# Second half of the tokens, and the state model's input, transposed straight from DRAM, under a rewritten order of work

## The chip, the cores and the metric

The kernel runs on one core of one Trainium2 chip. A core has engines with instruction queues of their own: TensorE (PE; its weight loads are listed as PEld), VectorE (DVE), ScalarE (ACT), GpSimd (POOL) and SyncE (SP), which here issues nearly all DMAs. Each queue is worked off in order, and the engines meet through semaphores. The time is the device time of one execution in microseconds; a profiled execution gives a span from the first to the last instruction and a time of its own.

## The reference

Two independent models, whose outputs are laid side by side (2048 tokens, 448 columns each). The first is local attention: 16 heads of 28 columns, each token looking at 8 tokens at distances 0, 2, ... 14.

```python
qkv = (x @ wqkv).reshape(B, S, 3, H, Dh)            # S = 2048, H = 16, Dh = 28
idx = pos[:, None] - 2 * arange(8)[None, :]
logits = einsum("bhsd,bhswd->bhsw", q, k[idx]) * Dh ** -0.5   # masked where idx < 0
a = einsum("bhsw,bhswd->bhsd", softmax(logits), v[idx]).reshape(B, S, D) @ wo
```

The second is a state model with 448 complex states, a diagonal recurrence over the tokens:

```python
h = Lam_bar * h + x[t] @ B_bar.T
y = 2 * real(h @ Cmat.T) + x * Dskip
```

## The kernel before

The kernel is one stream of some 560 named steps, written out by hand in the string `ORDER` (L32 to L61). Each step calls a function of the same name; the loop at L885 emits them in that order, so the order of the string is the order of every engine's queue. `@` gives the PSUM banks of a step; a trailing `.` has an eviction done by ACT, a trailing `=` by DVE. Large letters are mostly work for PE, small letters for the others.

Attention. Tokens are in two units `u` of 1024, each of two halves `s` of 512. PE wants x with columns on the partitions, as `xT`: 448 columns are three tiles of 128 and a tail of 64. For unit 0, x is loaded by rows into `xbuf` (as `xnA`) and PE transposes it: XI (first 512 tokens), XA and XH (second 512 tokens; XH is the tail), evicted by xi, xa and xh. For unit 1, x is loaded by rows too (L155 to L157), and four DMA transposes (L171 to L173) go from there into `xT`. The two halves' tails share one tile: half 0 on partitions 0 to 63, half 1 on 64 to 127.

QK(u, m, k) multiplies `xT` with a feature group `m` of `wq`: even m is query, odd m is key, m = 6 what is left of both (collected in `wq6` by POOL). k = 0 is the three full tiles of both halves, six matmuls; k = 1 the pair of tails; whichever comes first begins the bank. QS does a group for one half alone, as the first matmuls of the kernel. qk and qh evict. V_ and v do the values. P (L379, DVE) multiplies queries with shifted keys, E_ (PE) sums the products per head; lt, TD (a DMA transpose), sma, smb, smc are the softmax. AL, al, ad, sp bring the weights into banded form by way of a scratch in DRAM, into `PT`; AV, av, W_, w, ow make and store the attention output.

State model. Tokens are in chunks of 4. `Bn` (rows of B) is transposed by one DMA into `BT` (step BD). `xTB` is x with columns on the partitions, for two pairs of positions in a chunk (`a`) and 512 chunks. Before, x is loaded by rows into `xnB`, packed so that a pair of tokens is seven tiles of 128 (`x_load`, L164 to L169 and L179), and step xt (L694) transposes 128 chunks at a time into `xTB`, which lies in `xbuf`, over the rows of A. BU(g, jp, k) multiplies `BT` with the pair jp of `xTB`. BR, z, UP and y carry the state inside a chunk, sa, sb and sd scan over the chunks (DVE), DN, dn, H_ and h bring the states back, C and c make the output and oc stores it, from `xnA`, again over `xbuf`. XR reloads x by rows into `xnB` for the Dskip term (xd). ty, tf and ts make the tables of sines, the steps pa to pg the constants, rb the rotations, ca and cs scale C.

SP's queue is: first loads of x and `wq` (L141 to L153), unit 1's rows, the first x_load, unit 1's four transposes, Bn, the second x_load; then from `ORDER` BD, the four xt, TD0, LC, XR, CD, TD1 and what follows. ACT issues three small loads and one piece of the weights' tail (`w_half` with `eng=ACT`).

Of the kernel before, what the change touches and what calls it, by code (L numbers as in the profile page):

```python
# [16 lines left out]
NT = 16  # L17
# [21 lines left out]
P051 v411. ts06 v410. P060 QK110@46 ts16 BD v110. ts26 P061 QK101 ty3 QK151@72 QK111 qk100. E_05 rb0 qk101. E_06  # L39
qk110. QK150 tf4 lt00 P100 V_401@31 qk151. V_501@45 V_500 rb3 qk150. xt1 ts04 P101 lt01 QK120@27 ts14 qk111. tf3  # L40
v501. QK140@06 xt0 v500. P110 ts03 QK121 P111 QK141 qk120. QK161@54 V_400 qk140. xt3 P120 ts13 qk121. QK160 v400.
P121 qk141. v401. E_10@20 xt2 ts23 P130 E_11 ts24 V_510@73 qh101. P131 qh110. qh111. E_12 TD0 qh100. P140 E_13 hc1
V_511 P141 v511. v510. LC BU301@61 BU201@45 P150 BU300 sma0 BU200 OZ z30. XR BU400@37 z20. P151 smb0 BU000@64 P160
BR31 P161 BU001 ci1. BU401 E_14 z00. E_15 ci2= CD1 z40. E_16 rb1 z31. BR21 BR01 lt11 BU500@63 ci0= CD2 z21. smc0
z01. BU211@10 ci3. CD0 BU311@54 BU501 BU310 lt10 z50. CD3 BR32 BR41 BU210 z41. xd3 TD1 z32. BR51 xd2 BR22 AL0@2 z51.
BR33 z22. BU100@67 al0= z33. xd0 ca3 ad0 BU011@53 BU111@12 BU101 sma1 OP pm3 BU010 z10. pm0 wo UP3 AL1@6 cs3 smb1
BR11 xd1 BR02 BU110 z02. smc1 z11. BR03 al1. BR12 BU510@57 z03. ad1 z12. pm1 sp0 ca6 UP0 BR13 BU600@61 z13. y3. y0.
cs6 UP1 BR23 BU601 y1. z23. BU511 sa0 BU411@43 z60. BR52 pm4 ca1 BU410 sp1 sb0 BR61 z52. BR42 BU611@26 ca2 BU610 pm2
sd0 z61. AX@5 z42. BR53 BR62 AL2@1 ax= z53. z62. cs1 DN0@4 UP5 adx UP2 al2. DN1@5 BR43 dn0 BR63 y2. dn1 AL3@2 ad2
z63. sa2 H_10@1 y5. H_20@4 z43. H_11@0 al3. UP6 UP4 H_21@5 y6. H_00@7 ad3 y4. H_01@2 AV011@6 ca4 h21 spx AV010@3 h20  # L50
AV030@5 h01 av011. sp2 AV000@4 av010. cs2 AV020@6 av030. sb2 AV021@2 av000. AV001@3 av020. AV031@5 sd2 av001. W_00@4
sp3 av031. av021. W_20@6 ca5 h11 DN2@3 W_01@5 h00 DN3@2 dn2 w20. W_10@0 dn3 w01. sa4 ow20 W_11@7 ow01 W_21@3 w11.
w10. H_03@6 h10 H_02@2 w00. H_22@5 cs4 W_30@7 w21. ow00 sb4 H_23@0 ow21 H_13@1 w30. W_31@4 ow10 ca0 ow30 h13 AV100@3
ow11 h03 AV110@7 sd4 AV111@1 av110. AV131@6 av111. AV101@7 h02 av131. AV121@1 sa6 av101. AV130@6 av121. AV120@2 cs0
av130. DN5@7 av100. cs5 W_71@1 av120. dn5 W_61@6 w31. sb6 w71. h23 H_05@3 ow31 W_51@2 w61. ow71 ow61 W_41@7 w51= h05
H_15@4 ow51 H_25@1 W_50@0 h15 sd6 DN4@6 W_60@2 w50. w41. W_40@3 ow50 w60= ow41 DN6@4 C32@0 w40. ow60 dn6 dn4 ow40
h25 H_06@7 H_16@2 H_04@3 h06 H_12@4 H_14@6 h04 W_70@1 c32 H_24@7 C31@3 h22 oc32 w70= h12 C33@0 ow70 c31 h14 oc31
H_26@5 C30@1 c33 h26 oc33 h24 C02@4 c30 oc30 C20@3 c02 C00@6 c20 h16 oc20 CH0@0 c00 C01@5 oc00 C11@7 c01 ch0 oc01
C12@1 oh0 oc02 C13@4 C22@3 C03@2 c22 c12 oc22 c13 C21@6 oc12 c11 oc13 oc11 C10@5 c21 c03 oc21 CH1@0 oc03 c10 ch1
# [4 lines left out]
def kernel(  # L64
# [54 lines left out]
    xbuf = keep.tile([128, NT * D], BF16, tag="xbuf")  # L119
    xnA = xbuf.rearrange("p (t d) -> p t d", d=D)  # L120
# [34 lines left out]
    xA1 = xbuf[:, 8 * D:].rearrange("p (t n) -> p t n", n=2 * D)  # L155
    for d0, d1, b, c in ((0, D, 8, 0), (D, 512, 12, 384), (512, 896, 12, 0)):
        SP.dma_start(xA1[:, :, d0:d1], xA_r[:, b:b + 4, c:c + d1 - d0])  # L157


    xnB = keep.tile([128, 4, T, D], BF16, tag="xnB")  # L160
    xP = xnB.rearrange("p c j d -> p c (j d)").rearrange("p c (a n) -> p c a n", a=2)
    xB_r = B_x[0].rearrange("(q p h a b) d -> h p q a b d", q=2, p=128, h=2, a=2)

    def x_load(hh):  # L164
        for d0, d1, b, c in ((0, D, 0, 0), (D, 512, 1, 384), (512, 896, 1, 0)):
            for q in range(2):
                SP.dma_start(xP[:, 2 * hh + q, :, d0:d1], xB_r[hh, :, q, :, b, c:c + d1 - d0])

    x_load(0)  # L169

    xT = s2.tile([128, 2, 7, 512], BF16, tag="xT")  # L171
    for t in range(4):
        SP.dma_start(xT[:, 1, :, 128 * t:128 * t + 128], xA1[:, t], transpose=True)  # L173

    Bn = s2.tile([128, G, 512], BF16, tag="Bn")
# [3 lines left out]
    x_load(1)  # L179
# [154 lines left out]
    @op  # L334
    def QK(u, m, k):
        p = two("qk", u, m)
        part(("qk", u, m), k,
             [[(p[s][:], wqk(m, slice(64 * s, 64 * s + 64), 3), xT[64 * s:64 * s + 64, u, 3]) for s in range(2)]] if k else
             [[(p[s][:], wqk(m, slice(0, 128), kt), xT[:, u, 4 * s + kt]) for s in range(2)]
              for kt in range(3)])  # L340

    @op
    def QS(m, s):

        p = ps()
        pp.setdefault(("qk", 0, m), {})[s] = p
        for kt in range(3):
            PE.matmul(p[:], wqk(m, slice(0, 128), kt), xT[:, 0, 4 * s + kt], start=(kt == 0), stop=False)  # L348
        PE.matmul(p[:], wqk(m, slice(64 * s, 64 * s + 64), 3), xT[64 * s:64 * s + 64, 0, 3], start=False, stop=True)
# [341 lines left out]
    xTB = xbuf.rearrange("p (a b c) -> p a b c", a=2, b=7)  # L691

    @op
    def xt(cb):  # L694

        SP.dma_start(xTB[:, :, :, 128 * cb:128 * cb + 128].rearrange("p a b c -> p (a b) c"),
                     xnB[:, cb].rearrange("p j d -> p (j d)"), transpose=True)
# [222 lines left out]
```

## Time and profile before

| | |
|---|---|
| time, median of 3 runs | 133.71 us (133.06 to 136.21) |
| time of the profiled execution | 132.89 us |
| its span | 130.7 us |
| PE busy | 125.4 us, 1067 matmuls |
| DVE busy | 113.4 us |
| ACT busy | 88.8 us |
| HBM read, written | 11.69 MB, 6.37 MB |
| granted clock | 1.00 |

The profile's page gives busy times over the span and in 40 slices of 3.27 us, each digit the busy share in tenths. The timeline lists instructions in order with start, time taken, engine, line, tile written and read, number of them, and, in square brackets, idle time before them with what ended it. Matmuls overlap, so that one of 0.38 us lets the next start after about 0.21. SPq rows are instructions that issue DMAs; their time is that of the issue, not of the transfer.

### The profile page before, as it was taken

The page shows a single profiled execution, that of the slowest core. Times are in us where ns is not written, and L with a number is a line of the kernel's source. Part 1 is how long each engine was busy: PE and PEld are TensorE (multiplying, and loading weights), DVE is VectorE, ACT ScalarE, POOL GpSimd, SP SyncE. Part 2 cuts the span into 40 slices and gives each one's busy share as a digit, 9 for nine tenths or more (in the row PEclk, how much of TensorE's full clock was granted, in tenths as well). Part 3 has the DMA queues.
Part 4 walks back from the last instruction along what each step waited for, and adds up shares of the span by engine and source line. Part 5 has one row for each costly group of instructions (what it writes and reads, how often), then busy time and mean ns, then how long its engine had stood idle before and what let it go on. Part 6 is the DMA issues. An engine that isn't in the chain of part 4 may idle for free.

```text
span 130.7 us, 2869 instructions
## 1 busy us (share of the span) xinstructions
PE 125.4 (96%) x1067; PEld 62.2 (48%) x1067; DVE 113.4 (87%) x206; ACT 88.8 (68%) x185; POOL 19.8 (15%) x37
## 2 busy tenths in 40 slices
PE   6999999999999999999999999999899999999991
PEld 6543443434233334334454356854575555565550
DVE  5679999999999999999999899999997999752282
ACT  1779999999978996995979999997497300000000
POOL 6802000000000000200799920000000000000000
PEclk9999999999999999999999999999999999999999
DMA  3997989899999998999786999999412332213043
GB/s 116 238 207 174 326 230 167 197 197 258 139 259 210 212 200 187 310 303 209 209 200 222 185 169 293 255 179 185 141 54 70 105 105 94 87 55 103 0 146 118
DMA packets 47780, 23.24 MB, mean 178 GB/s; under 512 B 35639, under 2 KB 46711, under 8 KB 47767
## 3 DMA queue, kind: packets, MB, share of 16 engines
q1 hardware_dynamic: 47560, 23.03, 78.3%
q8 instruction: 8, 0.13, 0.4%
q10 hardware_dynamic: 207, 0.04, 0.2%
q14 instruction: 5, 0.04, 0.1%
HBM read 11.69 MB, written 6.37 MB: 138 GB/s over the span
## 4 chain that ended last, share of the span: by engine, by line
PE 80%; ACT 7%; DMA 6%; SPq 3%; issue 1%; DVE 0%; ACTq 0%
PE ps L244 38%; PE ps L807 15%; PE ps L547 6%; PE ps L534 5%; PE ps L391 5%; ACT ctmp L684 4%; DMA out_dram<-ya 3%; PE ps L722 3%; DMA wq<-in_A_wqkv_dram 3%; PE ps L788 3%; ACT Z L114 2%; SPq L128 2%; PE ps L348 1%; PE ps L827 1%; PE ps L395 1%
## 5 line engine op out<-in xcount | busy, mean ns | idle before, releaser
L379 DVE TENSOR_TENSOR pr<-qf,kf 128x2048 bf16<-128x2048 bf16 x24 | 28.7, 1236 | 0.1
L244 PE MATMUL ps<-xbuf,BT 128*128 128x512 bf16 (+1 forms) x112 | 23.6, 380 | 0.0
L244 PE MATMUL ps<-xT,wq 128*128 128x512 bf16 (+1 forms) x96 | 20.6, 380 | 0.1
L807 PE MATMUL ps<-Cw,Z 128*128 128x448 bf16 x105 | 20.5, 352 | 0.0
L114 ACT CAST Z<-ps 128x512 bf16<-128x512 f32 (+1 forms) x35 | 15.8, 520 | 3.0 <-PE ps L722 1.5
L813 DVE TENSOR_TENSOR xbuf<-ps,xnB 128x448 bf16<-128x448 f32 x15 | 9.0, 620 | 7.6 <-PE ps L807 7.5
L244 PEld LDWEIGHTS <-BT 128*128 128x128 bf16 (+1 forms) x112 | 8.9, 97 | 12.6 <-issue 3.5
L807 PEld LDWEIGHTS <-Z 128*128 128x128 bf16 x105 | 10.3, 98 | 9.4
L793 DVE TENSOR_TENSOR Z<-ps,Z 128x512 bf16<-128x512 f32 x21 | 13.7, 680 | 0.2 <-PE ps L788 0.2
L547 PE MATMUL ps<-wo,oT 128*128 128x448 bf16 x64 | 13.6, 353 | 0.0
L244 PEld LDWEIGHTS <-wq 128*128 128x128 bf16 (+1 forms) x96 | 7.8, 97 | 11.0 <-issue 2.3
L244 PE MATMUL ps<-wq,xT 128*128 128x448 bf16 (+1 forms) x64 | 13.0, 354 | 0.0
L877 POOL MEMSET PT<- 128x4320 f32 x3 | 11.0, 3698 | 7.2 <-DVE xnB L797 7.2
L114 ACT CAST ya<-ps 128x448 bf16<-128x448 f32 (+1 forms) x14 | 7.0, 566 | 5.5 <-PE ps L547 2.8
L684 ACT ACTIVATE ctmp<-Cw,c2t 64x448 f32<-64x448 bf16 x14 | 9.3, 667 | 0.3
L547 PEld LDWEIGHTS <-oT 128*128 128x128 bf16 x64 | 6.2, 98 | 5.7 <-ACT oT L114 0.2
L534 PE MATMUL ps<-PT,v_s 128*32 128x135 bf16 (+1 forms) x256 | 8.8, 298 | 0.0
L114 ACT CAST oT<-ps 128x512 bf16<-128x512 f32 x17 | 8.7, 620 | 0.1
L244 PEld LDWEIGHTS <-xT 128*128 128x128 bf16 (+1 forms) x64 | 4.8, 97 | 7.5 <-issue 4.1
L114 ACT CAST v_s<-ps 128x448 bf16<-128x448 f32 x16 | 8.2, 542 | 0.1
L534 PEld LDWEIGHTS <-v_s 128*32 128x32 bf16 x256 | 7.0, 110 | 0.7 <-ACT Z L114 0.4
L114 ACT CAST kf<-ps 128x512 bf16<-128x512 f32 x12 | 6.7, 582 | 0.7 <-PE ps L244 0.7
(150 smaller groups left out, 180.9 us busy)
## 6 DMA issues: line engine op xcount, KB each, us to landing
PT<-pd SPq DMA_DIRECT2D x16, 156.0 KB, 5.2
xnB<-in_B_x_dram SPq DMA_DIRECT2D x2, 896.0 KB
out_dram<-ya SPq DMA_DIRECT2D x16, 112.0 KB, 1.7
out_dram<-xbuf SPq DMA_DIRECT2D x15, 112.0 KB, 1.7
pd<-Ak SPq DMA_DIRECT2D x2, 640.0 KB, 3.5
xbuf<-in_A_x_dram SPq DMA_DIRECT2D x2, 448.0 KB
xnB<-in_B_x_dram SPq DMA_DIRECT2D x4, 224.0 KB, 5.4
xnB<-in_B_x_dram SPq DMA_DIRECT2D x4, 192.0 KB, 4.0
```

The lines of the kernel that those rows point to most:

```text
L114: (ACT.copy if e == "A" else V.tensor_copy)(o, i)
L244: PE.matmul(o, l, r, start=(first and i == 0), stop=(not first and i == len(pairs) - 1 and not more[s]))
L379: V.tensor_tensor(t[:], q.unsqueeze(1).to_broadcast((128, 4, 512)), k4, ALU.mult)
L391: PE.matmul(acc[s][32 * i:32 * i + 32], E[:, f, ws, :], t[:, i, :], start=(f == 0 and ws == 0), stop=False)
L534: PE.matmul(p[32 * hh:32 * hh + 32, 128 * bl:128 * bl + n], v_s[:, t, 4 * hg + hh, :], PT[:, t % NS, (4 * hg + hh) // HS, (4 * hg + hh) % ...
L547: PE.matmul(p[:, 0:D], late["oT"][:, b // 4, hg, par, 128 * (b % 4):128 * (b % 4) + 128], late["wo"][:, hg, :], start=(hg == 0), stop=(hg ...
L684: ACT.activation(t[a:a + 64, 0:D], Cw[b:b + 64, g, :], ACTF.Copy, scale=c2t[a:a + 64, g:g + 1])
L722: PE.matmul(pp["z", g, j][:], rot(g, 0), late["Z"][:, g, j - 1, :], start=False, stop=True)
L793: V.tensor_tensor(zz, pp.pop(("h", j, g))[:], zz, ALU.add)
L807: PE.matmul(p[:, 0:D], z, Cw[:, g, :], start=(g == 0), stop=(g == G - 1))
L813: V.tensor_tensor(yo, pp.pop(("c", j, ct))[:, 0:D], xnB[:, ct, j, :], ALU.add)
L877: POOL.memset(late["PT"][:, 4 * i:4 * i + 4].rearrange("p t g n -> p (t g n)").bitcast(F32), 0.0)
```

## The change

- Unit 1's x is no longer loaded by rows. `t_load` transposes 512 rows at a stride straight from DRAM, in three DMAs: 512 columns from the row's start (four tiles; the last has the row's tail of 64 columns on partitions 0 to 63, and 64 columns of the next row, which are not used), the three full tiles of a second row, and that row's columns 320 to 447 (the tail on partitions 64 to 127).
- The state model's x comes the same way, without x_load: each step xt now makes one half of the chunks (256) for one pair of positions `a = cb % 2`, in three DMAs. `xTB` and `xT` have eight tiles where they had seven, the second half's tail in the eighth (index `3 + 4 * s`).
- `xnA` (rows of unit 0) and `Bn` move into the place of `xnB`, which XR fills later; outputs of c go to `xbuf` as `yob`; the work tiles of ty and tf move to another pool.
- The weights' first load has 256 query columns in one DMA (before: 128 query and 128 key columns in two); keys follow in one load of all columns. Up to the last weight SP issues twelve DMAs (three of x, nine of weights) instead of sixteen.
- The first matmuls are QS for m = 0 and 2 (two query groups), not 0 and 1. `ORDER` is written anew, banks included. The evictions qk051, xa11, ci1 and av121 go from ACT to DVE; qk021, ci2, al0, ax, w60 and w70 from DVE to ACT.

```diff
 ORDER = """
-WU@0 XI0@0 xi00= xi01. XI1@1 XI2@2 xi10= xi11. PP@3 xi20. pcopy pa QS00@4 pb QS10@5 qk000. pd_ pc XH1@6 pe XA10@7
-xh1. XA11@1 qk010. xa10= QK021@32 xa11. QK031@04 P000 ty0 QS01@6 pf QS11@5 P001 QK051@71 QK030 tf0 qk011. qk001. pg
-ts00 QK050 qk031. ts10 ts20 QK020 qk051. P010 qk050. ty5 V_010@56 ty2 tf5 qk020. QK061@41 P011 V_001@73 ts05 V_011
-V_000 v010. qk030. tf2 ts15 QK060 qk021= ts25 v000. P020 v001. QK040@50 qh001. rb2 v011. qh011. QK041 V_111@27 ty1
-P021 V_101@36 V_110 qk040. qk041. tf1 ts02 E_00@50 P030 E_01 ts01 ts12 E_02 qh000. V_100 P031 qh010. v111. P040
-QK130@41 ts22 ts11 v101. P041 v100. V_411@76 ts21 QK131 E_03 hc0 P050 ty6 E_04 ty4 V_410 qk131. tf6 qk130. QK100@31
...
+WU@0 XI0@0 xi00= xi01. XI1@1 XI2@2 xi10= xi11. PP@3 xi20. QS00@4 pcopy pa pb QS20@5 pd_ pc pe XH1@6 qk000. XA10@7
+ty5 XA11@0 xh1. xa10= ty0 QK051@13 xa11= pf QK011@24 tf5 QS01@6 QS21@7 tf0 qk020. QK010 pg qk021. ts05 ts00 V_010@05
+qk011. ts15 qk001. rb3 QK050 qk010. ts10 P000 ts25 QK040@74 qk050. ty2 qk051= ts20 V_001@62 P001 QK041 QK031@13
+qk041. V_011 V_000 ty1 tf2 v010. v011. rb0 QK030 v000. ts02 P010 QK060@40 qk031. ts12 tf1 ts22 V_100@56 qk030. P011
+ts01 qk040. V_101 P020 QK061 ty6 V_111@31 V_110 v001. v101. tf6 v100. QK131@72 ts11 P021 QK130 v110. v111. qh001.
+P030 E_00@65 qh000. E_01 qk130. P031 QK111@31 qh010. V_410@47 ts06 ts21 P040 qk131. E_02 qh011. E_03 P041 ts16 V_411
+hc0 QK101@20 ty4 QK110 P050 v411. BD ts26 tf4 QK100 ty3 qk111. P051 QK150@71 qk101. tf3 v410. qk110. QK120@04 P060
+ts03 qk100. ts04 P061 QK121 xt2 QK151 QK161@32 qk151. E_04 P100 qk150. E_05 qk120. E_06 P101 qk121. QK160 xt0 lt01
+lt00 P110 V_511@17 ts13 E_10@04 ts14 qh101. P111 V_500@56 qh111. xt1 qh110. P120 V_510 qh100. ts24 P121 QK141@23
+v510. V_501 xt3 E_11 v501. P130 QK140 P131 V_400@16 TD0 qk140. v511. rb2 qk141. E_12 hc1 E_13 P140 v500. V_401 LC
+BU301@27 v401. BU201@35 BU200 P141 v400. ts23 sma0 BU300 OZ z20. XR BR21 BU400@61 z30. P150 smb0 BU000@32 ci0= P151
...
-    w_half(0, 0, 128, 0, D, eng=ACT)
+    w_half(0, 0, 256, 0, eng=ACT)
     SP.dma_start(xnA[:, 0:2], xA_r[:, 0:2])
     SP.dma_start(xnA[:, 2:4], xA_r[:, 2:4])
-    w_load(0, 128, 0, D)
+    w_load(0, 256, 0)
     SP.dma_start(xnA[:, 4:8], xA_r[:, 4:8])
-    w_half(1, 0, 256, 0, D)
-    w_load(128, 128, 0, D)
-    w_half(0, 128, 128, 0, D)
-    w_load(256, 192, 0, D)
-    for s in range(2):
-        w_half(s, 256, 192, 0, D)
+    w_load(0, D, D)
+    w_half(1, 0, D, 0, D)
+    w_half(0, 0, D, D)
+    w_load(256, 192, 0)
+    w_half(0, 256, 192, 0)
     w_load(0, D, 2 * D)
     for s in range(2):
         w_half(s, 0, D, 2 * D)
-    xA1 = xbuf[:, 8 * D:].rearrange("p (t n) -> p t n", n=2 * D)
-    for d0, d1, b, c in ((0, D, 8, 0), (D, 512, 12, 384), (512, 896, 12, 0)):
-        SP.dma_start(xA1[:, :, d0:d1], xA_r[:, b:b + 4, c:c + d1 - d0])
-    x_load(0)
-    for t in range(4):
-        SP.dma_start(xT[:, 1, :, 128 * t:128 * t + 128], xA1[:, t], transpose=True)
+    def t_load(x, off, step, row, n, out):
+        for k, b, o in ((4, 0, 0), (3, 4, step), (1, 7, step + 320)):
+            SP.dma_start(out[:, b:b + k], bass.AP(x.tensor, x.offset + off + o, [[row, n], [1, 128 * k]]), transpose=True)
+    t_load(A_x, 1024 * D, 512 * D, D, 512, xT[:, 1])
...
-    x_load(1)
...
     @op
     def xt(cb):
-        SP.dma_start(xTB[:, :, :, 128 * cb:128 * cb + 128].rearrange("p a b c -> p (a b) c"),
-                     xnB[:, cb].rearrange("p j d -> p (j d)"), transpose=True)
+        h, a = cb // 2, cb % 2
+        t_load(B_x, (T * h + 2 * a) * D, D, 2 * T * D, N2, xTB[:, a, :, N2 * h:N2 * h + N2])
```

More of the change, by code (lines that the diff above doesn't have):

```diff
@@ L38 @@
-QK130@41 ts22 ts11 v101. P041 v100. V_411@76 ts21 QK131 E_03 hc0 P050 ty6 E_04 ty4 V_410 qk131. tf6 qk130. QK100@31
[L39 to L57, printed above, removed]
@@ new lines @@
+lt00 P110 V_511@17 ts13 E_10@04 ts14 qh101. P111 V_500@56 qh111. xt1 qh110. P120 V_510 qh100. ts24 P121 QK141@23
+v510. V_501 xt3 E_11 v501. P130 QK140 P131 V_400@16 TD0 qk140. v511. rb2 qk141. E_12 hc1 E_13 P140 v500. V_401 LC
+BU301@27 v401. BU201@35 BU200 P141 v400. ts23 sma0 BU300 OZ z20. XR BR21 BU400@61 z30. P150 smb0 BU000@32 ci0= P151
+BR31 z21. BU001 P160 BU401 E_14 z00. z31. E_15 CD0 ci1= z40. BU500@53 P161 ci3. CD1 ci2. BR01 smc0 BR41 BU210@76
+z41. CD2 z01. E_16 BU501 CD3 lt11 BU211 BU311@12 lt10 BR22 BU310 z50. TD1 xd0 z22. AL0@4 xd1 BR51 BR32 al0. BR23
@@ new lines @@
+AL1@0 z32. xd3 ad0 BU100@57 z51. al1. rb1 z23. ad1 BR33 ca3 BU011@41 OP pm3 BU111@30 sma1 BU101 BU010 pm0 wo z33.
+z10. xd2 UP2 smb1 UP3 BR02 BR11 BU110 cs3 z02. smc1 z11. BR03 y2. BR12 y3. BU600@54 pm1 z12. sp0 z03. ca6 UP0 BR13
+BU510@76 z13. y0. cs6 UP1 BU601 y1. BU611@23 BU511 z60. sa0 BU411@10 pm4 BR52 sp1 AL2@5 z52. BU410 ca2 sb0 BR42 pm2
+AX@7 z42. BR61 sd0 BR53 BU610 z61. al2. z53. ad2 BR43 cs2 UP5 DN1@1 z43. DN0@4 BR62 ax. dn1 AL3@5 z62. dn0 H_11@7
+H_01@1 al3. H_20@4 h11 BR63 y5. H_10@2 ad3 h01 UP4 z63. H_00@5 adx H_21@6 y4. UP6 h10 ca4 AV010@7 sp2 sa2 AV020@1
@@ new lines @@
+AV001@0 y6. av010. AV000@2 av020. h21 AV030@3 av000. AV011@7 sb2 spx av001. AV021@1 av030. AV031@6 av011. sd2 W_00@2
+sp3 av031. av021. W_30@0 ca1 h20 W_31@3 cs4 DN2@7 W_20@6 w31. cs1 w30. DN3@1 ow31 W_21@4 ca0 dn3 ow30 dn2 W_11@3 sa4
+w20. H_13@0 H_03@1 w21. W_01@7 ow20 w11. h00 H_02@6 w00. H_23@4 ow11 W_10@3 h13 ow00 sb4 ow21 H_22@5 H_12@2 w10.
+AV120@0 w01. ow10 h02 ca5 AV101@3 ow01 h22 AV111@7 sd4 AV100@6 av101. AV121@5 av120. av100. AV131@3 av111. av121=
+AV110@0 av131. h23 AV130@6 av110. sa6 DN5@7 DN4@5 av130. W_71@3 dn5 W_60@4 dn4 sb6 W_61@0 w60. cs0 W_41@6 w61. cs5
@@ L60 @@
+H_04@7 ow61 H_15@5 w41. W_40@4 h04 w71. ow41 h03 W_70@0 sd6 H_24@6 H_14@7 w70. W_50@3 h12 W_51@1 h15 w50. DN6@0 h24
+H_25@2 ow50 C32@3 dn6 h14 h25 H_06@5 H_16@6 H_26@0 C31@7 h16 c32 H_05@2 C12@6 h05 c31 C33@3 h06 oc31 h26 c12 C11@2
+c33 oc12 oc33 C20@7 c11 ow60 ow70 oc11 C22@5 c20 ow71 oc32 oc20 C03@0 c22 w40. oc22 C21@6 ow40 c03 w51= oc03 CH0@3
+ow51 C02@2 C13@7 c02 c21 oc02 ch0 C01@5 oc21 c13 oh0 oc13 C30@4 c01 oc01 C00@0 c30 oc30 C10@1 c00 oc00 CH1@2 c10 ch1
 oc10 oh1
@@ L117 @@
     V.memset(wz[:], 0.0)
-    xbuf = keep.tile([128, NT * D], BF16, tag="xbuf")
-    xnA = xbuf.rearrange("p (t d) -> p t d", d=D)
+    xbuf = keep.tile([128, 16 * 512], BF16, tag="xbuf")
+    yob = xbuf[:, 0:8 * D].rearrange("p (t d) -> p t d", d=D)
+    xnB = keep.tile([128, 4, T, D], BF16, tag="xnB")
+    xn = xnB.rearrange("p c j d -> p (c j d)")
+    xnA = xn[:, 0:8 * D].rearrange("p (t d) -> p t d", d=D)
+    Bn = xn[:, 8 * D:].rearrange("p (g d) -> p g d", d=512)
     xA_r = A_x[0].rearrange("(t p) d -> p t d", p=128)
@@ L153 @@
         w_half(s, 0, D, 2 * D)
-    xA1 = xbuf[:, 8 * D:].rearrange("p (t n) -> p t n", n=2 * D)
-    for d0, d1, b, c in ((0, D, 8, 0), (D, 512, 12, 384), (512, 896, 12, 0)):
[L157 to L167, printed above, removed]
-    x_load(0)
-    xT = s2.tile([128, 2, 7, 512], BF16, tag="xT")
-    for t in range(4):
-        SP.dma_start(xT[:, 1, :, 128 * t:128 * t + 128], xA1[:, t], transpose=True)
-    Bn = s2.tile([128, G, 512], BF16, tag="Bn")
+    xT = s2.tile([128, 2, 8, 512], BF16, tag="xT")
+    def t_load(x, off, step, row, n, out):
+        for k, b, o in ((4, 0, 0), (3, 4, step), (1, 7, step + 320)):
+            SP.dma_start(out[:, b:b + k], bass.AP(x.tensor, x.offset + off + o, [[row, n], [1, 128 * k]]), transpose=True)
+    t_load(A_x, 1024 * D, 512 * D, D, 512, xT[:, 1])
     for d0, d1, c in ((0, D, 0), (D, 512, 384)):
@@ L337, in QK @@
         part(("qk", u, m), k,
-             [[(p[s][:], wqk(m, slice(64 * s, 64 * s + 64), 3), xT[64 * s:64 * s + 64, u, 3]) for s in range(2)]] if k else
+             [[(p[s][:], wqk(m, slice(64 * s, 64 * s + 64), 3), xT[64 * s:64 * s + 64, u, 3 + 4 * s]) for s in range(2)]] if k else
              [[(p[s][:], wqk(m, slice(0, 128), kt), xT[:, u, 4 * s + kt]) for s in range(2)]
@@ L348, in QS @@
             PE.matmul(p[:], wqk(m, slice(0, 128), kt), xT[:, 0, 4 * s + kt], start=(kt == 0), stop=False)
-        PE.matmul(p[:], wqk(m, slice(64 * s, 64 * s + 64), 3), xT[64 * s:64 * s + 64, 0, 3], start=False, stop=True)
+        PE.matmul(p[:], wqk(m, slice(64 * s, 64 * s + 64), 3), xT[64 * s:64 * s + 64, 0, 3 + 4 * s], start=False, stop=True)
     @op
@@ L641, in ty @@
     def ty(g):
-        pp["fr", g] = keep.tile([128, N2], F32, tag="fr", name="fr", bufs=2)
+        pp["fr", g] = s2.tile([128, N2], F32, tag="fr", name="fr", bufs=2)
         ACT.activation(pp["fr", g][:], iot[:], ACTF.Identity, scale=fT[:, g:g + 1])
@@ L646, in tf @@
     def tf(g):
-        kM, fr = keep.tile([128, N2], F32, tag="kM", name="kM")[:], pp["fr", g][:]
+        kM, fr = s2.tile([128, N2], F32, tag="kM", name="kM")[:], pp["fr", g][:]
         V.tensor_scalar(kM, iot[:], fT[:, g:g + 1], MAGIC, ALU.mult, ALU.add)
@@ L712, in BU @@
         part(("bu", g, jp), k,
-             [[(p[s][:], BT[64 * s:64 * s + 64, g, 3, :], xTB[64 * s:64 * s + 64, jp, 3, :]) for s in range(2)]] if k else
+             [[(p[s][:], BT[64 * s:64 * s + 64, g, 3, :], xTB[64 * s:64 * s + 64, jp, 3 + 4 * s, :]) for s in range(2)]] if k else
              [[(p[s][:], BT[:, g, f, :], xTB[:, jp, 4 * s + f, :]) for s in range(2)] for f in range(3)],
@@ L810, in c @@
     def c(j, ct):
-        yo = pp["yo", j, ct] = xnA[:, late["m"] % 8]
+        yo = pp["yo", j, ct] = yob[:, late["m"] % 8]
         late["m"] += 1
@@ L833, in ch @@
         if i == 0:
-            pp["yo"] = xnA[:, late["m"] % 8]
+            pp["yo"] = yob[:, late["m"] % 8]
             late["m"] += 1
```

8 lines of the change are left out of this document (3 added, 5 removed).

## The prediction

> **What bounds the kernel now.** First the page: busy time and slices.
>
> ```profile
> span 130.7 us, 2869 instructions
> PE 125.4 (96%) x1067; PEld 62.2 (48%) x1067; DVE 113.4 (87%) x206; ACT 88.8 (68%) x185; POOL 19.8 (15%) x37
> ...
> PE   6999999999999999999999999999899999999991
> ...
> DVE  5679999999999999999999899999997999752282
> ...
> DMA  3997989899999998999786999999412332213043
> ```
>
> PE is full from the second slice to the last but one. DVE is full too, up to about 95 us, and the DMA engines up to 92 us. Busy is not bound, so next the sums by stretch, which separate who has slack where (length, PE, PEld, DVE, ACT, POOL busy, clock, DMA share, GB/s):
>
> ```profile
> 0.00:10.00 10.00, 8.39 (x70) 5.55 (x71) 6.59 (x22) 5.40 (x15) 4.90 (x29) 1.00 0.74 184
> 10.00:48.00 38.00, 38.00 (x264) 14.74 (x262) 37.09 (x59) 36.11 (x81) 0.78 (x1) 1.00 1.07 214
> 48.00:80.00 32.00, 31.94 (x244) 14.22 (x241) 30.61 (x50) 28.12 (x54) 14.15 (x7) 1.00 0.97 220
> 80.00:113.00 33.00, 32.24 (x411) 19.57 (x411) 31.30 (x64) 19.16 (x38) 0.00 (x0) 1.00 0.58 143
> ```
>
> PE has 1.6 us idle before 10 us and 0.8 us between 80 and 113. So the span is a start, then 118 us of matmuls in a row (9.87 to 127.79), then 2.9 us of last eviction and store. Only a shorter start, fewer small pauses, or fewer matmuls can shorten it. Now the start, from PE's timeline:
>
> ```profile
> 6.69 0.82 PE L348 MATMUL ps<-xT,wq 128*128 128x512 bf16 x3
> 7.44 0.39 PE L349 MATMUL ps<-xT,wq 64*128 64x512 bf16 x1
> 8.02 0.41 PE L319 MATMUL ps<-ident,xbuf 128*64 128x128 bf16 x4 [0.19 <-DMA xbuf<-in_A_x_dram]
> 8.36 0.84 PE L305 MATMUL ps<-ident,xbuf 128*128 128x128 bf16 x12
> 9.33 0.61 PE L244 MATMUL ps<-xT,wq 64*128 64x512 bf16 x4
> 9.87 0.82 PE L348 MATMUL ps<-xT,wq 128*128 128x512 bf16 x3
> ```
>
> Here PE waits for x (8.02) and for a late piece of the weights (9.33; the chain of waits passes 3.69 us of that load). From 9.87 it does not wait for a load, save about 0.3 us at 11.9, until 92.5. Last, SyncE's queue, which issues the transfers that the change replaces:
>
> ```profile
> 10.55 1.69 SPq L157 DMA_DIRECT2D xbuf<-in_A_x_dram  x3
> 12.29 4.54 SPq L167 DMA_DIRECT2D xnB<-in_B_x_dram  x6
> 17.94 5.35 SPq L173 DMA_TRANSPOSE xT<-xbuf  x4
> ...
> 26.04 4.51 SPq L167 DMA_DIRECT2D xnB<-in_B_x_dram  x6
> 31.11 5.15 SPq L672 DMA_TRANSPOSE BT<-Bn  x1
> 36.30 8.11 SPq L696 DMA_TRANSPOSE xbuf<-xnB  x4
> ```
>
> These end at 23.3 and 44.4 us; their readers on PE start at 26.46 (QK130) and 47.76 (BU301). Both are late, but neither is waited for.
>
> **The change, part by part.**
>
> *Matmuls.* The steps of the two orders are the same, except that QS20 and QS21 replace QS10 and QS11 (with their QK counterparts): the same four-matmul form. PE's work changes by 0.
>
> *Start.* QS00's last matmul waits for xi20 on ACT (6.33) as before. QS20 needs only query columns from the first load, so it goes on at 6.6 instead of 6.69. The x of tokens 512 to 1023 is issued one DMA (0.5 us) earlier, 2.4 instead of 2.91; XH1 can then start at 7.6 instead of 8.02, when QS20's last matmul is issued. XH1, XA10, XA11 take 1.15 us to their end (8.02 to 9.21 less overlap), so the first key tails (QK051) come at 8.8. Their weights are now the sixth and seventh SyncE DMAs, issued by 5.1; the row of before took 3.7 us (issue 5.60, used 9.33), which gives 8.8. QS01 then waits for xa10 on DVE (8.55 plus 0.69) and starts at 9.25 against 9.87: **-0.6 us**. The 0.3 us pause at 11.9, for key and query columns loaded in pieces, goes too, as keys come in one load issued at 3.1: **-0.3 us**. If these loads, now larger, land as late as before, both are 0; if the start loses all its waits, they are -1.3 together.
>
> *Who is late next.* P000 needs qk010, and QK010 now follows QS21. ACT's queue is the longer path: qk000 to 7.86, ty5, xh1, ty0 to 9.2, table load 1.28, pf 0.7 (11.2), then eight entries to qk010, with QK010 itself done at 12.3: about 14.9. So P000 starts at 14.9, not 9.77. DVE fills that with xa11 (0.42), tf5 and tf0 (0.78 each), pg (2.31), rb3 (1.0): work that before stood behind P000. Behind P000 (1.14) stands qk051, evicted by DVE, done at 16.7; PE's QK031 needs that bank and comes up at 16.7. I take 0, with 0 to 0.5 us as bounds. Evictions moved between engines give DVE -1.22 us (out: qk021 0.68, ci2 0.45, al0 0.69, ax 0.40, w60 and w70 0.62 each; in: xa11, qk051 0.68, ci1 0.45, av121 0.69) and ACT about +0.9, of which most falls after 80 us, where it is busy 19 of 33. DVE is thus some 1.8 us ahead of its old time in the middle; the pairs I summed by rows (E_16 behind P161, AL0 behind smc0, H_11 behind dn1) keep 0.5 to 1.1 us: 0.
>
> *Transfers removed and added.* Gone from SyncE: 1.69 + 5.35 + 4.54 + 4.51 + 8.11 = 24.2 us of issue, and 2.7 MB of loads. Four weight DMAs fewer (2.3 us) bring the first transpose to 8.2. What a transpose out of DRAM costs, no row shows. From SBUF, seven 128x128 squares take 1.33 us of issue (0.19 each), fourteen 2.03 (0.145), twenty-eight 5.15. As the other end I take a lone Cw transpose, 2.7 us from issue to landing for seven squares (0.39). I take 0.19, since the packets are 256 B either way, and 256 B loads of wq from DRAM took 18 to 22 ns each, as those of the transposes did (20 to 23).
> Tokens: 32 squares, 6.1 us, 8.2 to 14.3, landed 2.1 later (the old ones: issue ended 23.3, last packets 24.9 and the signal): **16.4**. QK131, now first on them, comes after 14.1 us of matmuls that ran 1.07 times that long before (QS01 to QK130): 9.25 + 15.1 = **24.3**. Cover 7.9 us.
> State model: Bn 2.7 to 17.0, landed 21.7, BT 5.15 to 26.9, then xt2 and xt0, the only halves that BU301 and BU201 read, 6.1 to 33.0, landed **35.1**; PE reaches BU301 at 47.76 - 0.9 = **46.9**. Cover 11.8 us. So 10 us less of a full DMA is worth 0: PE did not wait for it.
> New waits: the reload of xnB (XR) waits for BT's read of Bn, some ten us earlier; outputs in xbuf wait for BU's reads, over by 72. Nothing queues there. For the pause of 0.68 us at 92.5 (PT from the scratch) I count 0, bounds -0.7 and 0; for pauses that a new order makes or removes elsewhere, -1.5 to +2 (the flagged pauses of before sum to about 3 us after 9.87).
>
> At 0.39 a square, the bound, both covers shrink: 0.39/0.19 = 2.05 times 6.1 gives 22.8 for the tokens (still covered) and 47.9 for BU301, 1.0 us late.
>
> [...]
>
> **Sum.** 132.89 (profiled execution: span 130.7 and 2.2 around it) - 0.6 - 0.3 = 132.0. The runs' median, 133.71, stands 0.8 higher; less 0.9 it is 132.8. I give 132.4, between them.
>
> **Rivals.**
> 1. *DRAM transposes are slow* (slower than before). With k times 0.19 a square, tokens land at 10.3 + 6.1k and BU's half at 22.9 + 12.2k. The second passes 46.9 from **k = 2.0**, the first 24.3 from 2.3. At 2.5: 1.3 late, then 5.2 more: 132.0 + 6.5 = **138.5**. For it: rows of 896 B, no row of a transpose from DRAM. Against it: equal packet times. Chance 0.09. [...]
> 2. *The late P000 or a new pause eats the gain.* DVE and ACT have no gap from 12 to 48 us; if qk010 lands at 16.5 instead of 14.9, QK031 waits 1.6 us, and the total is **133.6**; two such places, 135. It decides from P000 later than about 15. For it: 37.1 and 36.1 us busy of 38. Against it: DVE's 1.22 us less. Chance 0.24.
> 3. *More pauses go.* The start's full 1.3 and about 1.5 of the 3 us: **130.1**. For it: transfers ten us earlier. Against it: few of those pauses end by a DMA. Chance 0.11.
> The forecast, 131.2 to 133.6, has 0.56.
>
> **Numbers.** The range leaves out rival 1 and the ends of 2 and 3: 130.3 to 135.4. 2% (2.7 us) is about what a measurement tells here, the three runs spreading 133.06 to 136.21. Below 131.0: rival 3, 0.11. Above 136.4: rival 1, 0.09. Within: 0.80.
>
> **What would show it.** First L348 of QS01 near 9.25; first pr near 14.9; the transposes' issue ended near 14.3 and 39, without a PE wait on xT or xbuf at QK131 and BU301; DMA slices less full before 45 us; PE busy unchanged at 125 us; last CH near 126.9. A wait of PE for xT, or DVE gaps beyond 1 us between 15 and 60, would make it wrong.

## The result: 0.7% longer, and the profile after

The changed kernel took 133.81 us (median of 20 executions, 132.81 to 134.93), the kernel before 132.84 us on the same chip (20 executions): a ratio of 1.0071, 95% interval 1.0051 to 1.0090. That is about 0.95 us more, inside the 2% that counts as no change; the forecast was 0.9 us less (132.4, range 130.3 to 135.4). Times in this document are medians of all executions, ratios and their intervals are of the means without executions more than 1.5% above the fastest of their kernel, so that the two can differ.

Two profiled executions of the changed kernel exist, of 134.93 us (span 133.0) and 134.16 us (span 132.2). The views below are of the second, since the first is the longest of the 20 executions; it shows the same picture with QS01 0.8 us later. First the page, busy times and slices.

```profile
span 132.2 us, 2837 instructions
...
PE 126.5 (96%) x1058; PEld 62.6 (47%) x1067; DVE 111.9 (85%) x204; ACT 90.5 (68%) x187; POOL 19.7 (15%) x37
...
PE   6899999999999999999999999999999999999990
...
PEclk9999999999999999999999999999999999999999
DMA  3999992997698799764698994999520210373321
```

PE is full from the third slice to the last but one; DVE fell by 1.5 us, and the DMA engines now have air in most slices from 7 to 20. PE is busy 1.1 us longer, with the same steps. By stretch (length, PE, PEld, DVE, ACT, POOL busy, granted clock, DMA share, GB/s):

```profile
0.00:10.00 10.00, 8.38 (x49) 4.78 (x49) 5.67 (x20) 4.41 (x13) 4.92 (x29) 1.00 0.80 216
10.00:48.00 38.00, 37.46 (x255) 15.00 (x259) 35.59 (x59) 34.71 (x76) 0.61 (x1) 1.00 0.88 157
48.00:80.00 32.00, 31.62 (x239) 13.82 (x242) 29.88 (x47) 28.09 (x53) 14.17 (x7) 1.00 0.83 197
80.00:113.00 33.00, 32.92 (x428) 20.27 (x428) 31.80 (x67) 22.72 (x45) 0.00 (x0) 1.00 0.51 125
```

In the first 10 us PE is as busy as before (8.38 against 8.39 us) but has started 49 matmuls where it had started 70. What is lost is lost there: the same busy time with fewer matmuls. Between 80 and 113 us the change gained: 32.92 us busy against 32.24. The start in PE's timeline:

```profile
5.67 0.24 PE L564 MATMUL ps<-ident,raw 7*128 7x7 bf16 x3
6.32 1.46 PE L340 MATMUL ps<-xT,wq 128*128 128x512 bf16 x3 [0.42 <-DMA wq<-in_A_wqkv_dram]
7.71 0.60 PE L341 MATMUL ps<-xT,wq 64*128 64x512 bf16 x1
8.25 1.46 PE L340 MATMUL ps<-xT,wq 128*128 128x512 bf16 x3
9.65 0.50 PE L341 MATMUL ps<-xT,wq 64*128 64x512 bf16 x1
10.08 0.41 PE L311 MATMUL ps<-ident,xnB 128*64 128x128 bf16 x4
...
11.20 0.60 PE L236 MATMUL ps<-xT,wq 64*128 64x512 bf16 x4
```

Two things stand here that the profile of before did not have. QS00 (the first L340) waits 0.42 us for the first weights, which is now one load of 256 columns. And a row of three 512-column matmuls takes 1.46 us, where before it took 0.82: with the last one's 0.6 and 0.38 us taken off, the starts lie 0.42 us apart instead of 0.22. So PE works at half rate here, up to about 9.9 us. The granted-clock row says 1.00 and 9 throughout and does not show this. The trace's own clock records do: the first one, of the full clock, begins at 9.92 us, and the views count the time ahead of it as 1.00. In the first profile of after it begins at 10.76, in that of before at 4.66. The spacing in the first profile of before agrees: 0.107 us between 128-column matmuls until some 4.6 us, 0.056 after it.

The kernel before has this too: a second profile of it (shown below) has the half rate up to 7.3 us. The comparison of the two kernels by points on PE's timeline (QS01 is the first group after the start, C the last step; QS01 is read from its first weight load, which can stand 0.1 us ahead of the first matmul; times in us):

| | QS00 | next QS | XH1 | key tails QK051 | QS01 | last C ends | QS01 to last C | span |
|---|---|---|---|---|---|---|---|---|
| before, first profile | 5.50 | 6.69 | 8.02 | 9.33 | 9.87 | 127.79 | 117.92 | 130.7 |
| before, second profile | 5.85 | 7.59 | 8.66 | 9.78 | 10.32 | 128.43 | 118.11 | 131.3 |
| after, first profile | 7.02 | 8.95 | 10.85 | 11.97 | 12.50 | 129.86 | 117.36 | 133.0 |
| after, second profile | 6.32 | 8.25 | 10.08 | 11.20 | 11.73 | 129.10 | 117.36 | 132.2 |

Between the two second profiles the sum closes: QS00 0.47 us later; from QS00 to XH1 3.76 us instead of 2.81, the half rate lasting longer, 0.95; the rest of the start equal. That makes QS01 1.41 us late. The stretch from QS01 to the end of C is 0.75 us shorter, and what lies behind it (last store) 0.3 us longer: 0.96 us, as the spans say (132.23 less 131.26).

### The profile page after: what moved, and what is told of

Read it like the earlier page. It is cut to its first block, busy times and chain, and to the rows that moved or that the text cites. A ratio compares the mean times of both kernels' runs of the same rounds, so it can differ in the third digit from the quotient of the medians.

```text
span 133.0 us, 2837 instructions
## 1 busy us (share of the span) xinstructions
PE 126.5 (95%) x1058; PEld 62.6 (47%) x1067; DVE 112.0 (84%) x204; ACT 90.4 (68%) x187; POOL 19.7 (15%) x37
## 3 DMA queue, kind: packets, MB, share of 16 engines
HBM read 8.94 MB, written 6.37 MB: 115 GB/s over the span
## 4 chain that ended last, share of the span: by engine, by line
PE 78%; ACT 11%; DMA 4%; DVE 3%; issue 1%; SPq 1%
PE ps L236 31%; PE ps L799 15%; PE ps L539 6%; PE ps L526 6%; DMA wq<-in_A_wqkv_dram 4%; PE ps L714 3%; PE ps L340 3%; PE ps L383 3%; PE ps L780 3%; DVE pr L371 3%; ACT ctmp L676 2%; ACT ya L114 2%; ACT kf L114 2%; PE ps L341 1%; ACT fr L635 1%; ACT v_s L114 1%
## 5 line engine op out<-in xcount | busy, mean ns | idle before, releaser
L371 DVE TENSOR_TENSOR pr<-qf,kf 128x2048 bf16<-128x2048 bf16 x24 | 28.1, 1218 | 0.2 <-ACT kf L114 0.2
L114 ACT CAST Z<-ps 128x512 bf16<-128x512 f32 (+1 forms) x35 | 16.3, 509 | 2.0 <-PE ps L236 0.7
L114 ACT CAST ya<-ps 128x448 bf16<-128x448 f32 (+1 forms) x16 | 8.0, 541 | 13.3 <-DMA out_dram<-ya 9.7
L114 ACT CAST qf<-ps 128x512 bf16<-128x512 f32 x12 | 6.9, 591 | 3.2 <-PE ps L341 1.6
L114 ACT CAST oT<-ps 128x512 bf16<-128x512 f32 x16 | 8.2, 628 | 0.0
```

The source lines that it names most:

```text
L114: (ACT.copy if e == "A" else V.tensor_copy)(o, i)
L371: V.tensor_tensor(t[:], q.unsqueeze(1).to_broadcast((128, 4, 512)), k4, ALU.mult)
```

## The experiments

The theory: all of the loss is in the start, and its parts are (a) the first weights, one load of 192 KB instead of two of 96 KB, land later, and with them the key tails, and (b) the wait this gives PE (1.12 and 0.42 us in the two profiles) falls into the time at half rate and prolongs it. The rivals: the DMA transposes out of DRAM cost the time somewhere, or the new order makes pauses of its own. Every kernel here computes the whole output; matmuls that are added work on zeros and their product is not used. Each ratio is to the kernel before, run beside it on the same chip.

### The two kernels once more

No edit.

> The changed kernel, unaltered, for a second profile beside the ones that follow. Theory (the start): the first weight load, now 192 KB in one DMA, lands late; in the profile on record it let PE start at 7.02 us instead of 5.50, and after the pause eight matmuls took 0.41 us each instead of 0.25; from QS01 (12.50, before 9.87) to the last C the changed kernel is 0.6 us quicker. It expects QS00 at 6.3 to 7.0 and QS01 at 11 to 12.5 here, and a ratio to the kernel before of 1.005 to 1.010. Rival (the long stretch): the loss lies in pauses after QS01, spread over the new order; then QS01 is near 10 in this profile and the stretch from it to the end is over 118.5 us.

> The kernel before, unaltered, for a second profile of its start. In the first one PE changed from 0.107 to 0.056 us between starts of 128-column matmuls at 4.56 us, and QS00 began at 5.50. [...] Rival (the load alone): full rate at 4.5 to 4.7 again, as the instructions before it are the same.

After: 134.09 us (133.99 to 135.35, 4 executions), ratio 1.0109 (1.0061 to 1.0156). Before, one execution: 133.47 us. PE's timeline of the kernel before, in this second profile:

```profile
5.85 1.46 PE L348 MATMUL ps<-xT,wq 128*128 128x512 bf16 x3
7.25 0.42 PE L349 MATMUL ps<-xT,wq 64*128 64x512 bf16 x1
7.59 0.82 PE L348 MATMUL ps<-xT,wq 128*128 128x512 bf16 x3
```

QS00 at half rate (1.46), QS10 at full (0.82): full rate from about 7.3 us, where the first profile of this kernel had it by 5.5. The theory had full rate anywhere from 4.5 to 7.5 us and QS01 at 9.8 to 10.6 (measured: 10.32). The end of the half rate thus falls in another place in these two executions of one kernel, and a single profile must not be read as the kernel's start. The profile that the prediction was made from was one of the good ones.

### The DRAM transposes alone

The kernel before, its order and weight loads kept, with the new transfers of x and the moves of buffers that go with them; in short:

```diff
+    t_load(A_x, 1024 * D, 512 * D, D, 512, xT[:, 1])
-    x_load(0)
-    x_load(1)
```

> The transposes straight from DRAM alone: order of work and weight loads are those of before, x for tokens 1024 to 2047 and for the state model as in the changed kernel. Theory: transposes from DRAM cost PE nothing, so the time is that of before within 0.5 us (132.3 to 133.3), the start is that of before (QS00 at 5.5, QS01 at 9.9), and PE waits neither for xT nor for xbuf. Rival (the transposes slow something, by their own time or by what they take from others): 133.5 or more, with pauses after QS01 that the kernel before does not have.

133.04 us (132.56 to 133.93, 10 executions), ratio 1.0004 (0.9978 to 1.0031). QS01 at 10.47, QS01 to last C 117.91: close to the kernel before in both. Within the interval (0.3 us less to 0.4 more) the transposes cost nothing and bring nothing, though HBM reads fall from 11.69 to 8.94 MB. So the first rival falls.

### The new order and weight loads with the old x

The kernel before with the new `ORDER` and the new weight loads, x still by rows.

> The other half of the change alone: new order of work and new weight loads, but x of tokens 1024 to 2047 and of the state model by rows and from there transposed, as before. Theory (the loss is in the first weight load and what PE's clock does after it): as slow as the changed kernel, ratio to the kernel before 1.005 to 1.011, QS00 at 6.3 to 7.0. Rival (the transposes from DRAM cost something that only the new order shows, for instance by transfers that now run beside the start): ratio 0.995 to 1.000.

135.34 us (133.96 to 136.52, 4 executions), ratio 1.0133 (1.0057 to 1.0209). PE's timeline:

```profile
6.56 0.82 PE L347 MATMUL ps<-xT,wq 128*128 128x512 bf16 x3 [0.85 <-DMA wq<-in_A_wqkv_dram]
...
10.71 0.69 PE L243 MATMUL ps<-xT,wq 64*128 64x512 bf16 x4 [0.83 <-DMA wq<-in_A_wqkv_dram]
```

The loss is there without any DRAM transpose of x, and both waits are for weights: 0.85 us for the first load, 0.83 for the key tails. In this execution full rate had come at 5.22 us, ahead of the wait, and was kept: its 133.96 us, 0.9 over the median of before, hold the late loads without a late half rate. The stretch behind QS01 is 117.32 us, so the 0.6 us gained there are the new order's too. Two of the four executions (135.9 and 136.5) are longer than the start can explain; what they spent it on no profile shows.

### Only the first load cut in two

The changed kernel, with

```diff
-    w_load(0, 256, 0)
+    w_load(0, 128, 0)
+    w_load(128, 128, 0)
```

> Only the first weight load is parted again: two DMAs of 128 query columns each (96 KB) instead of one of 256 (192 KB). Theory (size of the first load): QS00 starts at 5.5 again, no half-speed matmuls, QS01 near 10, time 1.5 to 2.5 us under the changed kernel, about 131.5 to 132.3, and under the kernel before. Rival (the load is late because of what is queued with it, not its size): QS00 stays at 6.3 to 7.0, and the time within 0.5 us of the changed kernel's.

133.42 us (132.63 to 135.55, 10 executions), ratio 1.0027 (0.9999 to 1.0056). By the ratios that is 0.6 to 1.1 us under the changed kernel, less than the 1.5 to 2.5 expected. In its profile:

```profile
6.01 0.82 PE L341 MATMUL ps<-xT,wq 128*128 128x512 bf16 x3
...
10.00 0.69 PE L237 MATMUL ps<-xT,wq 64*128 64x512 bf16 x4 [0.66 <-DMA wq<-in_A_wqkv_dram]
```

No wait ahead of QS00, and full rate from it on. By the ratios the larger part of the loss is gone (0.36 us left of some 0.95 to 1.45). What is late next is the tails' weights, by 0.66 us.

### Also the key tails ahead of the keys

In addition, the tails' loads go ahead of the load of all keys:

```diff
-    w_load(0, D, D)
     w_half(1, 0, D, 0, D)
     w_half(0, 0, D, D)
+    w_load(0, D, D)
```

> The changed kernel with the first load in two (as in the run with the parted load) and the two loads of the keys' tails issued ahead of the keys' main rows, which are needed 2.7 us later. In the run with the parted load QK051 waited for these tails until 10.00, 0.8 us. Theory: that wait goes, QS01 at 9.7 to 10.0, time 0.6 to 0.9 us under that run, 132.4 to 132.9, so 0 to 0.5 us under the kernel before. Rival (the start is worth nothing, since a later engine sets the pace): the gain shows at QS01 and is given back by pauses after it; time as with the parted load, 133.2 to 133.6.

132.72 us (132.12 to 134.08, 12 executions), ratio 0.9969 (0.9936 to 1.0003).

```profile
5.98 0.82 PE L341 MATMUL ps<-xT,wq 128*128 128x512 bf16 x3 [0.36 <-DMA wq<-in_A_wqkv_dram]
...
8.69 0.41 PE L312 MATMUL ps<-ident,xnB 128*64 128x128 bf16 x4 [0.49 <-DMA xnB<-in_A_x_dram]
...
9.81 0.61 PE L237 MATMUL ps<-xT,wq 64*128 64x512 bf16 x4
```

The wait for the tails is gone; x is now late by 0.49 us; why is open, since in the run before, with the same DMAs ahead of it, it had landed by 8.16. The kernel stands some 0.4 us below the kernel before, at the edge of what this run can tell. The order of a few loads at the start is thus worth more (about 1.3 to 1.9 us from the changed kernel to this one, by the ratios) than what the new order gains behind QS01 (0.6 to 0.75).

### The wait bridged with matmuls on zeros

The changed kernel, loads as changed, with a step WV ahead of QS00: 24 matmuls of 128 columns in the one run, 8 in the other.

```diff
+    @op
+    def WV():
+        p = ps()
+        for _ in range(24):
+            PE.matmul(p[:, 0:128], wz[:], wz[:], start=True, stop=True)
```

> The changed kernel with 24 further matmuls on zeros between PP and QS00, so that PE is not idle while it waits for the weights; the load is as in the changed kernel. Theory (the pause itself slows the matmuls after it): QS00's and QS20's matmuls follow each other in 0.21 to 0.25 us instead of 0.41, QS01 is 1.0 to 1.6 us earlier, time 1.0 to 1.5 us under the changed kernel although the weights land as late. Rival (they are slow because transfers into SBUF get in their way): still 0.41 us, and no gain, or a loss of up to 1 us where the added matmuls last longer than the wait.

> The changed kernel with 8 further matmuls on zeros between PP and QS00, which last 0.45 to 0.85 us and so end before the weights land (6.3 to 7.0). The load stays one DMA of 192 KB. [...]

With 24: 134.16 us (133.39 to 135.71, 7 executions), ratio 1.0079 (1.0043 to 1.0115), so the gain of 1.0 to 1.5 us did not come, and its profile (134.83 us) also loses 0.8 us behind QS01, with waits at 71 and 88 us (0.44 and 0.26) that no other profile here has. With 8: 133.84 us (132.93 to 134.19, 12 executions), ratio 1.0039 (1.0009 to 1.0069). PE's timeline with 8:

```profile
5.83 0.81 PE L262 MATMUL ps<-wz 128*128 128x128 bf16 x8
6.98 0.82 PE L347 MATMUL ps<-xT,wq 128*128 128x512 bf16 x2 [0.33 <-DMA wq<-in_A_wqkv_dram]
...
8.05 0.82 PE L347 MATMUL ps<-xT,wq 128*128 128x512 bf16 x3
...
11.01 0.69 PE L236 MATMUL ps<-xT,wq 64*128 64x512 bf16 x4 [0.70 <-DMA wq<-in_A_wqkv_dram]
```

Expected with 8 were a ratio of 1.000 to 1.005 and QS matmuls 0.22 us apart, or, if the half rate does not come from the wait, 1.007 to 1.011 and 0.41. The weights land as late as in the changed kernel (6.98; 7.02 in its first profile), yet both QS groups run at full rate (0.22 us between starts), from about 6.3 us; with 24 matmuls the rate turns at 6.3 us, but they last until 7.38, past the landing, and QS00 waits for them instead. PE now waits for the key tails, which by the signals in the traces landed at 10.96 us here and at 10.88 with 24. In the two profiles of the changed kernel the same loads landed at 9.75 and 10.84, and PE, at half rate, came to them only at 11.20 and 11.97. So there the half rate set the start, here the tails do, and which of them costs more hangs on an execution's landings. The times do not tell the two apart: by the ratios the kernel with 8 is 0.4 to 0.9 us under the changed one, but the intervals overlap, and the medians (133.84 against 133.81 and 134.09) show next to nothing. What the half rate costs the changed kernel on average is thus not measured; that the late loads cost time without it (0.5 us by this ratio) is.

### Cut, load and bridge together

> The kernel with the parted first load and the tails ahead of the keys' main rows, and 4 further matmuls on zeros between PP and QS00 (0.23 to 0.43 us, in a wait of 0.36 us there). [...]

The kernel with both reorderings of loads, and four matmuls on zeros ahead of QS00: 132.52 us (132.20 to 132.74, 12 executions), ratio **0.9952** (0.9925 to 0.9979); expected were 132.4 to 132.8 and 0.994 to 0.998. It lies 0.5% under the kernel before, inside the 2% but with an interval clear of 1.

```profile
5.60 0.40 PE L263 MATMUL ps<-wz 128*128 128x128 bf16 x4
5.87 0.82 PE L348 MATMUL ps<-xT,wq 128*128 128x512 bf16 x3
...
9.33 0.61 PE L237 MATMUL ps<-xT,wq 64*128 64x512 bf16 x4
9.95 0.81 PE L348 MATMUL ps<-xT,wq 128*128 128x512 bf16 x3
```

QS01's first weight load stands at 9.86, 117.36 us ahead of the end of C; the span is 130.3. Full rate came at 5.12 us, ahead of the bridge, so this profile does not show what the bridge is worth. The executions spread over 0.54 us, those of the kernel with the tails moved alone over 1.96 (0.76 without the longest).

### The kernel before with the same bridge

> The kernel before with the same 4 further matmuls on zeros between PP and QS00, to see what the quickest run so far owes to them and what to the new order. [...] Rival (the matmuls give the gain, the new order nothing): 132.5, ratio 0.994 to 0.997, as the quickest run.

Four matmuls on zeros ahead of QS00 in the kernel before: 133.02 us (132.66 to 134.75, 13 executions), ratio 1.0003 (0.9980 to 1.0026). The bridge alone brings nothing there (expected: within 0.3 us, 0.998 to 1.002), so the 0.5% of the run above go with the new order behind QS01 (117.36 us, where the two profiles of before have 117.92 and 118.11). The profiled execution is the longest of the 13, 134.75 us:

```profile
6.01 0.60 PE L270 MATMUL ps<-wz 128*128 128x128 bf16 x4
6.41 1.49 PE L355 MATMUL ps<-xT,wq 128*128 128x512 bf16 x3
7.83 0.60 PE L356 MATMUL ps<-xT,wq 64*128 64x512 bf16 x1
8.36 0.61 PE L355 MATMUL ps<-xT,wq 128*128 128x512 bf16 x1
```

Half rate until past 9.5 us (the clock record begins at 9.87), though PE had no wait for a load. This limits the theory, as far as one execution can, and the longest of its run: a wait is not needed for a late full rate.

### The first load of the kernel before made large

```diff
-    w_load(0, 128, 0, D)
+    w_load(0, 256, 0)
+    w_load(0, 128, D)
...
-    w_load(128, 128, 0, D)
+    w_load(128, 128, D)
```

> The kernel before with one thing of the changed one: its first weight load is 256 query columns (192 KB), then 128 key columns as a load of their own. Theory (the size of the first load): QS00 at 6.3 to 7.0 instead of 5.5 to 6.0, full rate only at 7 to 11, QS01 at 11 to 12.5, and 0.8 to 2.0 us slower than before (133.6 to 134.8). Rival (the new order's own queueing in the start): within 0.5 us of before.

133.45 us (132.69 to 135.25, 10 executions), ratio 1.0022 (0.9983 to 1.0060): the rival's size, within 0.5 us, not the 0.8 to 2.0 us that the theory asked for. The profile says why it is small in that execution:

```profile
4.77 0.41 PE L285 MATMUL ps<-ident,xbuf 128*64 128x128 bf16 x4
...
6.75 0.82 PE L349 MATMUL ps<-xT,wq 128*128 128x512 bf16 x3 [1.41 <-DMA wq<-in_A_wqkv_dram]
```

The load lands at 6.7, as late as in the changed kernel, though the load of x behind it is issued at 2.91 us as in the kernel before: the larger load does that, in the old order too. But full rate had come ahead of the wait (the four transposes at 4.77 take 0.41 us, where in the second profile of after four take 0.64), and 1.41 us of idle time did not take it away; and the key tails, whose loads are where they were, were not late (QK051 at 10.00).

### Fewer matmuls on zeros at the very start

The kernel before begins with 22 of them (WU).

```diff
-        for _ in range(22):
+        for _ in range(4):
```

> The kernel before with 4 instead of 22 matmuls on zeros at its start; no load and no other step changes. Theory (PE runs at half rate until it has been busy long enough): QS00 still begins at 5.5 to 6.1, full rate comes at 8 to 11 instead of 4.6, the QS matmuls follow each other in 0.43 us, QS01 1 to 1.5 us later, time 0.8 to 1.5 us over before. Rival (half rate in the changed kernel came from its transfers): no change, within 0.3 us.

135.37 us (133.78 to 135.92, 4 executions), ratio 1.0100 (1.0032 to 1.0169), with no load touched.

```profile
3.52 1.57 PE L288 MATMUL ps<-ident,xbuf 128*128 128x128 bf16 x12 [1.85 <-DMA xbuf<-in_A_x_dram]
...
5.76 1.46 PE L348 MATMUL ps<-xT,wq 128*128 128x512 bf16 x3
...
7.69 1.46 PE L348 MATMUL ps<-xT,wq 128*128 128x512 bf16 x3
```

This is the picture of the changed kernel's start, with the loads of before: half rate up to about 9.2 us, QS01 at 11.10. The one thing taken out is work on zeros; in its place PE is idle for 1.85 us. So idle time in the first microseconds, without any load that lands later, makes the kernel about 1% longer by the ratio, and the half rate is what its profile shows for it. The two longest of the four executions have no profile.

## Why the prediction was wrong, step by step

**The bound: right.** PE in a row sets the time; the stretch behind the start went from 117.92 and 118.11 to 117.36 us. That is the gain the forecast had not counted. Most of it is the pause of 0.68 us at 92.5, costed at 0 with bounds of -0.7 and 0, and a second one behind it. In PE's timeline of before both end with an eviction by ACT, not with `PT` from the scratch as the prediction read it (the last piece of `PT` landed at 92.41):

```profile
93.70 0.19 PE L528 MATMUL ps<-PT,v_s 128*32 128x7 bf16 x4 [0.47 <-ACT ya L114]
...
95.68 0.19 PE L528 MATMUL ps<-PT,v_s 128*32 128x7 bf16 x4 [0.25 <-ACT oT L114]
```

After has no such wait (32.92 of 33 us busy). Nearly all that was lost lies in the start.

**The start, -0.6 and -0.3: wrong, and the failing step.** The prediction said that QS20 "needs only query columns from the first load, so it goes on at 6.6". It took the load of 256 columns to land when that of 128 did, and its bounds (0 to -1.3) allowed no loss. By the last of its signals in the traces, the load of 256 columns landed at 6.28 to 6.98 us in all six profiles that have it, that of 128 at 5.03 to 6.12 in the other eight. QS01 was to start at 9.25 and started at 11.73 and 12.50. The chain of waits of after shows it as its first long piece:

```profile
1.83 4.45 DMA wq<-in_A_wqkv_dram
6.32 1.46 PE ps L340 x3
```

The second failing step is in the same sum: the tails' weights, "the sixth and seventh SyncE DMAs", got the 3.7 us of the old row and 8.8 us. They landed at 9.75 and 10.84 us in the two profiles of after, behind the load of all keys, which was priced at nothing; where PE was at full rate it waited for them until 10.00 to 11.01. Moving that load behind the tails took the wait away. And x of tokens 512 to 1023, issued 0.5 us earlier, was to let XH1 start at 7.6; it landed at 7.74 and 8.73, in before at 7.98 and 7.91.

**The half rate: not in the sum at all.** The prediction took 0.22 us a matmul, from a profile in which full rate had come before QS00. In the profiles here it came anywhere between some 4.4 and 10.8 us, at 4.66 in that profile, which was luck. That PE at half rate is what the profiles of after show is measured (0.42 us between starts). That the wait for the load is its cause there is supported and not settled. The clock records last 122.88 or 126.29 us, a difference of 3.41; they are 36 and 37 times that. In each of the 13 profiles with such a record PE was idle for less than 0.3 us in the 3.41 us ahead of full rate. One such stretch earlier, the two profiles of after were idle for 0.57 and 1.12 us, by the wait in the main, and the run with 4 matmuls at the start for 1.13. The late case without a wait for a load (the kernel before with the bridge, 9.87 us) was idle for 0.15 there and does not fit. Where full rate had come ahead of the wait (the new order with the old x, the tails moved, the large first load in the kernel before), the wait (0.85, 0.36 and 1.41 us) did not undo it.

**P000: right in distance.** Foreseen 5.65 us behind QS01 (14.9 less 9.25), measured 5.70; QK031 did not wait, as taken. DVE's work fell from 113.4 to 111.9 us (foreseen: -1.22). DVE's timeline:

```profile
17.43 1.23 DVE L371 TENSOR_TENSOR pr<-qf,kf 128x2048 bf16<-128x2048 bf16 x1 [0.23 <-ACT kf L114]
```

**The transposes: hidden, as said; their price off in size.** SyncE's timeline:

```profile
8.97 5.15 SPq L165 DMA_TRANSPOSE xT<-in_A_x_dram  x3
...
21.70 4.25 SPq L664 DMA_TRANSPOSE BT<-xnB  x1
25.99 16.69 SPq L165 DMA_TRANSPOSE xbuf<-in_B_x_dram  x12
42.79 1.25 SPq L405 DMA_TRANSPOSE attn<-lt  x1
```

The tokens' three took 5.15 us and ended at 14.1 (foreseen 6.1, at 14.3). The state model's twelve took 16.69 us (foreseen 12.2, to 39; ended 42.7), since each takes 1.24 us or more, even for two squares: the term was mis-sized by taking 0.19 us a square where small ones have a floor. Neither was waited for (QK131 at 26.91, BU301 at 50.17; behind the latter is one gap of 0.16 us). The tokens' 32 squares took 0.16 us of issue each.

**DMA share:** 1.07 to 0.88 between 10 and 48 us, worth 0, as said and as the run of the DRAM transposes alone shows.

**The rivals.** The first (slow DRAM transposes) fell. The second, a new wait that eats the gain (133.6 us), came nearest to the time, but by luck: its place was wrong, not behind P000, but ahead of QS00 and the key tails. The third had its gain of pauses, about 0.6 us of it, and no shorter start. The prediction's ends do not meet: its range runs from 130.3 to 135.4, while its chances count what lies below 131.0 and above 136.4.

## What to carry to other kernels

When two loads at the head of a kernel become one, ask what waits for their first part: it now waits for the whole (here 6.28 to 6.98 us instead of 5.03 to 6.12), and so does what is queued behind the larger load (the key tails, at 9.75 and 10.84). Read PE's rate at the start from the spacing of its matmuls (here 0.42 us), not from the granted-clock row (1.00 all the same), in two or more profiles. When a change has parts that act in different stretches (here loads at the start, order behind it), run each alone: behind a total of +0.95 us lay, between two profiles, +1.4 at the start, -0.75 behind it and +0.3 at the last store, and the version that keeps the second and issues the first loads in smaller pieces and another order, with four matmuls on zeros, is below both kernels.

## What the runs showed of the hardware that was not expected

- PE's first matmuls run at half rate (0.107 us between 128-column, 0.42 between 512-column ones; 0.056 and 0.22 afterwards), until a point that fell between some 4.4 and 10.8 us in the profiles; in two of the kernel before, at 4.66 and 7.35. The granted-clock row reads 1.00 all the while, since the trace has no clock record ahead of full rate.
- A first load of 192 KB landed at 6.28 to 6.98 us (six profiles), one of 96 KB at 5.03 to 6.12 (eight), both issued at about 1.8 us. Whether size or the shape of its packets does it was not separated.
- In the first profile of after, the issue of a DMA transpose out of DRAM took 1.24 to 1.67 us for 2 to 12 squares of 128x128 and 2.02 for 16 (in the second, 1.24 to 2.17 and 2.30): a floor for each, then little per square.
- PE, idle for 1.41 us after full rate had come (the large first load in the kernel before), stayed at full rate: the next three 512-column matmuls took 0.82 us.
